# A fused attention and gated feed-forward kernel on one core: four 32-row matmuls at a time on TensorE, with a written-out order for every engine

## The chip, the cores and the metric

The chip is a Trainium2 and the kernel runs on one of its cores. The metric is the time on the device in microseconds (us), the median of several executions. "Clock" is the mean TensorE clock that the hardware granted, as a share of full speed. A run is called slow when it lies over 1.5 % above the fastest run of the same kernel.

## The reference

```python
B, N, m, C = (4, 12416, 32, 128)          # batches, tokens, inducing points, channels
d_ff = 1536                                # 12 chunks of 128

def mab(q, kv):
    s = scale * (q @ kv.transpose(0, 2, 1))
    s = s - s.max(-1, keepdims=True)
    a = np.exp(s)
    a /= a.sum(-1, keepdims=True) + 1e-09
    return a @ kv
h = mab(I, x)                              # stage 1: the 32 inducing points look at all tokens
x2 = mab(x, h)                             # stage 2: every token looks at the 32 rows of h
gate = 1.0 / (1.0 + np.exp(-(x2 @ w_gate)))
val = x2 @ w_val
out = gate * val @ w_out                   # 49664 x 128
```

Both kernels use that `x2` is a product of 128 tokens' weights over only 32 rows. They fold `h @ w_gate` and `h @ w_val` once a batch into a table of 32 rows ("fold"). The gate and value matmuls then contract over those 32 rows. The sigmoid is written with tanh: gate × value = 0.5 · (tanh(g/2) + 1) · v.

## The kernel before

It goes through each batch in blocks of 512 tokens: 24 full blocks and one of 128 tokens. A step is one tanh with the work around it: six steps make a full block, each for two of the twelve 128-wide chunks of d_ff. (With the change the short block has two steps, so there are 4 × (24 × 6 + 2) = 584 in all.) This is the core of a block, with cuts marked. The contraction is padded from 32 to 128 rows with zeros, and the output is transposed by a DMA.

```python
    pp_g = ...tile_pool(name="pp_g", bufs=2, space=PSUM)   # two double banks for gates
    pp_v = ...tile_pool(name="pp_v", bufs=3, space=PSUM)   # three banks for values and everything else
    pp_acc = ...tile_pool(name="pp_acc", bufs=1, space=PSUM)
    # ... (cut)
        for p in range(NP2):                       # six steps of two chunks
            j0, j1 = 2 * p, 2 * p + 1
            g_pair = pp_g.tile([P, 2, TOK], F32, tag="g")
            nc.tensor.matmul(
                g_pair[:, 0, 0:T], hwg[:, ts(j0, P)], a2[:, 0:T], start=True, stop=True
            )
            # ... the same for j1 (cut)
            nc.scalar.activation(
                out=tgs[:, 0:2, 0:T], in_=g_pair[:, 0:2, 0:T], func=AF.Tanh, scale=0.5
            )
            for (jj, j) in ((0, j0), (1, j1)):
                v_ps = pp_v.tile([P, TOK], F32, tag="v")
                nc.tensor.matmul(
                    v_ps[:, 0:T], hwv[:, ts(j, P)], a2[:, 0:T], start=True, stop=True
                )
                nc.vector.scalar_tensor_tensor(
                    out=u[:, 0:T], in0=tgs[:, jj, 0:T], scalar=1.0,
                    in1=v_ps[:, 0:T], op0=ALU.add, op1=ALU.mult,
                )
            for (j, u) in prev_us:
                nc.tensor.matmul(
                    acc_ps[:, 0:T], wo16[:, j, :], u[:, 0:T], start=(j == 0), stop=(j == NJ - 1),
                )
            # ... one piece of the attention work of another block goes here (cut)
        nc.scalar.copy(out=outT16[:, 0:T], in_=acc_ps[:, 0:T])
        nc.sync.dma_start(onat16[:, 0:nch, :], outT16[:, 0:T], transpose=True)
```

The softmax here doesn't subtract the row's maximum and nothing guards it: scores larger than these inputs give would overflow.

Of the kernel before, what the change touches and what calls it, by code (L numbers as in the profile page):

```python
# [14 lines left out]
P = 128  # L16
TOK = 512


def _affine_eye(nc, ap, pattern, fill=1.0):  # L20
    nc.gpsimd.memset(ap, 0.0)
    nc.gpsimd.affine_select(
        out=ap,
        in_=ap,
        compare_op=ALU.not_equal,
        fill=fill,
        base=0,
        pattern=pattern,
        channel_multiplier=1,
    )  # L30
# [3 lines left out]
def kernel(  # L34
# [11 lines left out]
    m = inducing.shape[0]  # L46
    F = moe_w_gate.shape[1]
    NJ = F // P
    SCALE = float(1.0 / (C ** 0.5))

    assert C == P and m == 32 and F % P == 0 and N % P == 0

    nfull = N // TOK
    tail = N - nfull * TOK
    blocks = [(i * TOK, TOK) for i in range(nfull)]
    if tail:
        blocks.append((nfull * TOK, tail))
    nb = len(blocks)

    const = ctx.enter_context(tc.tile_pool(name="const", bufs=1))  # L60
    xTp = ctx.enter_context(tc.tile_pool(name="xTp", bufs=2))
    pers = ctx.enter_context(tc.tile_pool(name="pers", bufs=1))
    hp = ctx.enter_context(tc.tile_pool(name="hp", bufs=2))
    xab = ctx.enter_context(tc.tile_pool(name="xab", bufs=16))
    a1p = ctx.enter_context(tc.tile_pool(name="a1p", bufs=2))
    a2rp = ctx.enter_context(tc.tile_pool(name="a2rp", bufs=3))
    moep = ctx.enter_context(tc.tile_pool(name="moep", bufs=4))
    outp = ctx.enter_context(tc.tile_pool(name="outp", bufs=4))

    pp_g = ctx.enter_context(tc.tile_pool(name="pp_g", bufs=2, space=bass.MemoryType.PSUM))  # L70
    pp_v = ctx.enter_context(tc.tile_pool(name="pp_v", bufs=3, space=bass.MemoryType.PSUM))
    pp_acc = ctx.enter_context(tc.tile_pool(name="pp_acc", bufs=1, space=bass.MemoryType.PSUM))

    ident128 = const.tile([P, P], F16, tag="ident128")
    _affine_eye(nc, ident128[:], [[-1, P]])

    ind16 = const.tile([m, C], F16, tag="ind16")
    nc.gpsimd.dma_start(ind16[:], inducing)
    indT16 = const.tile([P, m], F16, tag="indT16")
    nc.sync.dma_start(indT16[:], ind16[:], transpose=True)  # L80

    wg16 = const.tile([P, F], F16, tag="wg16")
    nc.gpsimd.dma_start(wg16[:], moe_w_gate)
    wv16 = const.tile([P, F], F16, tag="wv16")
    nc.gpsimd.dma_start(wv16[:], moe_w_val)
    wo16 = const.tile([P, NJ, C], F16, tag="wo16")
    nc.gpsimd.dma_start(wo16[:], moe_w_out.rearrange("(j p) c -> p j c", p=P))

    NPAD = 3
    a2pads = [pers.tile([P, TOK], F16, name=f"a2pad{k}", tag=f"a2pad{k}") for k in range(NPAD)]  # L90
    hwgs = [pers.tile([P, F], F16, name=f"hwg{q}", tag=f"hwg{q}") for q in range(2)]
    hwvs = [pers.tile([P, F], F16, name=f"hwv{q}", tag=f"hwv{q}") for q in range(2)]
    for t_ in (*a2pads, *hwgs, *hwvs):
        nc.vector.memset(t_[m : 2 * m, :], 0.0)
        nc.vector.memset(t_[64:P, :], 0.0)

    xTs = [xTp.tile([P, N], F16, tag="xT", name=f"xT_{b}") for b in range(B)]
    h16s = [pers.tile([m, C], F16, name=f"h16_{b}", tag=f"h16_{b}") for b in range(B)]
    hT16s = [pers.tile([P, m], F16, name=f"hT16_{b}", tag=f"hT16_{b}") for b in range(B)]
    haccs = [pers.tile([m, C + 4], F32, name=f"hacc_{b}", tag=f"hacc_{b}") for b in range(B)]  # L100
    for b in range(B):
        nc.vector.memset(haccs[b][:], 0.0)

    x16nats = {}
    a1s = {}

    def x16nat_load(b, kk):
        t0, T = blocks[kk]
        nch = T // P
        x16nat = xab.tile([P, 4, C + 4], F16, tag="x16nat")  # L110
        nc.gpsimd.dma_start(  # L111
            x16nat[:, 0:nch, 0:C],
            x[b, ds(t0, T)].rearrange("(j p) c -> p j c", p=P),
        )
        nc.vector.memset(x16nat[:, 0:nch, C : C + 1], 1.0)
        x16nats[(b, kk)] = x16nat

    def st1_a(b, kk, pe_xt):
        t0, T = blocks[kk]
        nch = T // P  # L120
        x16nat = x16nats[(b, kk)]
        xt_ps = pp_v.tile([P, TOK], F16, tag="v")
        for j in range(nch):
            nc.tensor.transpose(xt_ps[:, ts(j, P)], x16nat[:, j, 0:C], ident128[:])  # L124
        if pe_xt:
            nc.vector.tensor_copy(out=xTs[b][:, ds(t0, T)], in_=xt_ps[:, 0:T])
        else:
            nc.scalar.copy(out=xTs[b][:, ds(t0, T)], in_=xt_ps[:, 0:T])

    def st1_b(b, kk):  # L130
        t0, T = blocks[kk]
        nch = T // P
        s1_ps = pp_v.tile([P, 4, m], F32, tag="v")
        for j in range(nch):
            nc.tensor.matmul(  # L135
                s1_ps[:, j, :],
                xTs[b][:, ds(t0 + j * P, P)],
                indT16[:],
                start=True,
                stop=True,  # L140
            )
        a1 = a1p.tile([P, 4, m], F16, tag="a1")
        nc.scalar.activation(
            out=a1[:, 0:nch, :], in_=s1_ps[:, 0:nch, :], func=AF.Exp, scale=SCALE
        )
        a1s[(b, kk)] = a1

    def st1_c(b, kk):
        t0, T = blocks[kk]
        nch = T // P  # L150
        x16nat = x16nats.pop((b, kk))
        a1 = a1s.pop((b, kk))
        hpp = pp_v.tile([m, C + 1], F32, tag="v")
        for j in range(nch):
            nc.tensor.matmul(  # L155
                hpp[:],
                a1[:, j, :],
                x16nat[:, j, 0 : C + 1],
                start=(j == 0),
                stop=(j == nch - 1),  # L160
            )
        nc.vector.tensor_tensor(
            out=haccs[b][:, 0 : C + 1],
            in0=haccs[b][:, 0 : C + 1],
            in1=hpp[:],
            op=ALU.add,
        )

    def ab_end0(b):
        rec = hp.tile([m, 1], F32, tag="rec")  # L170
        nc.vector.reciprocal(out=rec[:], in_=haccs[b][:, C : C + 1])
        nc.vector.tensor_scalar_mul(
            out=h16s[b][:], in0=haccs[b][:, 0:C], scalar1=rec[:]
        )
        hT_ps = pp_v.tile([P, m], F16, tag="v")
        nc.tensor.transpose(hT_ps[:], h16s[b][:], ident128[0:m, 0:m])
        nc.vector.tensor_copy(out=hT16s[b][:], in_=hT_ps[:])

    def ab_fold(b, q):
        hwg, hwv = hwgs[b % 2], hwvs[b % 2]  # L180
        npg = F // TOK
        (dst, w, sc) = (hwg, wg16, None) if q < npg else (hwv, wv16, 0.5)
        ss = q % npg
        hw_ps = pp_v.tile([m, TOK], F32, tag="v")
        nc.tensor.matmul(
            hw_ps[:], hT16s[b][:], w[:, ts(ss, TOK)], start=True, stop=True
        )
        if sc is None:
            nc.vector.tensor_copy(out=dst[0:m, ts(ss, TOK)], in_=hw_ps[:])
        else:  # L190
            nc.vector.tensor_scalar_mul(  # L191
                out=dst[0:m, ts(ss, TOK)], in0=hw_ps[:], scalar1=sc
            )

    a2ns = {}

    def st2_a(b, i):
        t0, T = blocks[i]
        nch = T // P
        s2_ps = pp_v.tile([P, 4, m], F32, tag="v")  # L200
        for j in range(nch):
            nc.tensor.matmul(  # L202
                s2_ps[:, j, :],
                xTs[b][:, ds(t0 + j * P, P)],
                hT16s[b][:],
                start=True,
                stop=True,
            )
        a2r = a2rp.tile([P, 4, m], F16, tag="a2r")
        nc.scalar.activation(  # L210
            out=a2r[:, 0:nch, :], in_=s2_ps[:, 0:nch, :], func=AF.Exp, scale=SCALE
        )
        sums_tok = a2rp.tile([P, 4], F32, tag="sums_tok")
        nc.vector.reduce_sum(out=sums_tok[:, 0:nch], in_=a2r[:, 0:nch, :], axis=AX.X)
        rtok = a2rp.tile([P, 4], F32, tag="rtok")
        nc.vector.reciprocal(out=rtok[:, 0:nch], in_=sums_tok[:, 0:nch])  # L216
        a2n = a2rp.tile([P, 4, m], F16, tag="a2n")
        nc.gpsimd.tensor_tensor(  # L218
            out=a2n[:, 0:nch, :],
            in0=a2r[:, 0:nch, :],  # L220
            in1=rtok[:, 0:nch].unsqueeze(2).to_broadcast((P, nch, m)),
            op=ALU.mult,
        )
        a2ns[(b, i)] = a2n
# [196 lines left out]
```

## Time and profile before

| | before |
|---|---|
| median of 2 runs | 970.2 us (969.97 to 970.43) |
| span of the profiled run, clock | 967.2 us, 0.986 |
| busy: PE / DVE / ACT / POOL | 96 % / 88 % / 73 % / 20 % |
| chain that ended last | PE 92 % |

The engines are PE (TensorE's matmuls), PEld (its weight loads), DVE (VectorE), ACT (ScalarE), POOL (GpSimd) and SP (which issues DMAs). These are lines of the page of the kernel before: the busy line, the clock in 40 slices of the span (tenths of full speed), the chain that ended last by engine, and the largest groups. In a group, the first figures after the bar are the busy us and the mean ns of one instruction. Then come the idle us before them and what ended most of that idleness.

```profile
span 967.2 us, 16308 instructions
...
PE 932.7 (96%) x5568; PEld 423.7 (44%) x5568; DVE 855.0 (88%) x1779; ACT 701.6 (73%) x976; POOL 195.4 (20%) x310
...
PEclk9899999999999999999999999999999999999998
...
PE 92%; DVE 4%; DMA 1%; ACT 1%; issue 1%; POOL 1%; POOLq 0%; ACTq 0%; DVEq 0%
...
L264 DVE SCALAR_TENSOR_TENSOR u<-tgs,v_ps 128x512 f16<-128x512 f16 (+1 forms) x1200 | 746.5, 666 | 76.9 <-PE v_ps L260 37.6
L254 ACT ACTIVATE tgs<-g_pair 128x1024 f16<-128x1024 f32 x600 | 592.4, 1004 | 184.9 <-PE g_pair L250 126.5
L274 PE MATMUL acc_ps<-u,wo_104 128*128 128x512 f16 (+1 forms) x1000 | 357.4, 374 | 0.0
```

PE is busy throughout at nearly full clock, and the chain that ended last runs through it. The 374 ns of the output matmul are not its cost, since matmuls overlap in the pipeline. The cost is the distance between the starts. This is the timeline of PE (start, duration, engine, line, operation, out<-in):

```profile
501.44 0.38 PE L247 MATMUL g_pair<-a2pad_108,hwg_110 128*128 128x512 f16 x1
501.66 0.38 PE L260 MATMUL v_ps<-a2pad_108,hwv_112 128*128 128x512 f16 x1
```

The starts of such neighbours are 0.215 to 0.216 us apart in the whole trace. A block has 36 such matmuls, so 7.8 us of its some 9.4 us are these alone, although three quarters of the rows of the gate and value matmuls are zeros.

### The profile page before, as it was taken

How to read it: one execution, taken by the hardware profiler on the slowest of the kernel's cores; microseconds unless marked ns; L12 is line 12 of the kernel's file. 1: busy time of each engine (PE TensorE's matmuls, PEld its weight loads, DVE VectorE, ACT ScalarE, POOL GpSimd, SP SyncE). 2: the span in 40 equal slices, each digit the busy share in tenths (PEclk: the TensorE clock that was granted, in tenths of full speed). 3: DMA queues.
4: the chain of work that ended last, by engine and by line, in shares of the span. 5: the costliest groups of instructions: out<-in, count | busy, mean ns of one | idle time of the engine just before them, and what ended most of it. 6: DMA issues, size and time to landing. Idle time of an engine off the chain costs nothing.

```text
span 967.2 us, 16308 instructions
## 1 busy us (share of the span) xinstructions
PE 932.7 (96%) x5568; PEld 423.7 (44%) x5568; DVE 855.0 (88%) x1779; ACT 701.6 (73%) x976; POOL 195.4 (20%) x310
## 2 busy tenths in 40 slices
PE   4799999999989999999998999999998999999996
PEld 3444444444444444444444444444443544444443
DVE  6799889898889889898898988898888899999996
ACT  1277787777857787777866787777775787888884
POOL 8511221212211221212221121211110111111111
PEclk9899999999999999999999999999999999999998
DMA  9924434445533434444451435423232233233333
GB/s 152 118 36 53 61 50 57 58 52 66 64 40 45 61 50 56 61 52 63 61 66 27 55 51 59 56 39 45 39 45 34 37 50 49 39 50 49 47 48 54
DMA packets 157428, 53.12 MB, mean 55 GB/s; under 512 B 107424, under 2 KB 157088, under 8 KB 157344
## 3 DMA queue, kind: packets, MB, share of 16 engines
q0 software_dynamic: 104416, 39.34, 34.8%
q1 hardware_dynamic: 52928, 12.74, 7.3%
q8 instruction: 43, 0.70, 0.3%
q14 instruction: 41, 0.34, 0.1%
HBM read 27.80 MB, written 25.43 MB: 55 GB/s over the span
## 4 chain that ended last, share of the span: by engine, by line
PE 92%; DVE 4%; DMA 1%; ACT 1%; issue 1%; POOL 1%; POOLq 0%; ACTq 0%; DVEq 0%
PE v_ps L260 27%; PE acc_ps L274 21%; PE g_pair L247 15%; PE g_pair L250 13%; PE acc_ps L285 4%; PE a2nT_ps L233 3%; PE hpp L155 3%; PE xt_ps L124 2%; DVE u L264 2%; PE s_ps L135 2%; DMA x16nat<-in_x_dram 1%; PE s_ps L202 1%; ACT tgs L254 1%; DVE hwv_111 L191 0%; DVE hwv_112 L191 0%
## 5 line engine op out<-in xcount | busy, mean ns | idle before, releaser
L264 DVE SCALAR_TENSOR_TENSOR u<-tgs,v_ps 128x512 f16<-128x512 f16 (+1 forms) x1200 | 746.5, 666 | 76.9 <-PE v_ps L260 37.6
L254 ACT ACTIVATE tgs<-g_pair 128x1024 f16<-128x1024 f32 x600 | 592.4, 1004 | 184.9 <-PE g_pair L250 126.5
L274 PE MATMUL acc_ps<-u,wo_104 128*128 128x512 f16 (+1 forms) x1000 | 357.4, 374 | 0.0
L218 POOL TENSOR_TENSOR a2n<-a2r,rtok 128x128 f16<-128x128 f16 (+1 forms) x100 | 38.7, 387 | 531.9 <-DVE rtok L216 527.3
L274 PEld LDWEIGHTS <-wo_104 128*128 128x128 f16 x1000 | 97.6, 98 | 106.5 <-issue 11.4
L111 POOL DMA_DIRECT2D x16nat<-in_x_dram x100 | 73.7, 747 | 56.0 <-PE hpp L155 29.6
L260 PEld LDWEIGHTS <-hwv_112 128*128 128x128 f16 x600 | 56.7, 97 | 63.5 <-issue 6.1
L260 PEld LDWEIGHTS <-hwv_111 128*128 128x128 f16 x600 | 55.6, 98 | 56.0 <-issue 5.4
L285 PE MATMUL acc_ps<-u,wo_104 128*128 128x512 f16 (+1 forms) x200 | 74.5, 373 | 1.9 <-DVE u L264 1.9
L260 PE MATMUL v_ps<-a2pad_106,hwv_111 128*128 128x512 f16 (+1 forms) x216 | 75.7, 369 | 0.0
L260 PE MATMUL v_ps<-a2pad_106,hwv_112 128*128 128x512 f16 (+1 forms) x216 | 74.9, 363 | 0.3 <-DVE u L264 0.2
L260 PE MATMUL v_ps<-a2pad_108,hwv_111 128*128 128x512 f16 x192 | 70.0, 379 | 1.0 <-DVE hwv_112 L191 0.4
L260 PE MATMUL v_ps<-a2pad_108,hwv_112 128*128 128x512 f16 x192 | 69.6, 379 | 0.6 <-DVE u L264 0.4
L260 PE MATMUL v_ps<-a2pad_107,hwv_112 128*128 128x512 f16 x192 | 69.7, 379 | 0.0
L260 PE MATMUL v_ps<-a2pad_107,hwv_111 128*128 128x512 f16 x192 | 69.6, 379 | 0.0
L124 PE MATMUL xt_ps<-ident_91,x16nat 128*128 128x128 f16 x388 | 39.3, 224 | 13.6 <-DMA x16nat<-in_x_dram 11.8
L210 ACT ACTIVATE a2r<-s_ps 128x128 f16<-128x128 f32 (+1 forms) x100 | 28.9, 289 | 28.3 <-PE s_ps L202 27.9
L124 PEld LDWEIGHTS <-x16nat 128*128 128x128 f16 x388 | 29.9, 100 | 33.6 <-DMA x16nat<-in_x_dram 12.4
L250 PEld LDWEIGHTS <-hwg_109 128*128 128x128 f16 x300 | 29.4, 98 | 33.9 <-issue 11.2
L233 PE MATMUL a2nT_ps<-ident_91,a2n 128*32 128x128 f16 x388 | 39.9, 223 | 3.8 <-POOL a2n L218 1.9
L250 PEld LDWEIGHTS <-hwg_110 128*128 128x128 f16 x300 | 29.2, 97 | 32.1 <-issue 7.0
L247 PE MATMUL g_pair<-a2pad_106,hwg_109 128*128 128x512 f16 (+1 forms) x108 | 40.6, 376 | 1.6 <-DVE a2pad_106 L234 1.3
(610 smaller groups left out, 1051.3 us busy)
## 6 DMA issues: line engine op xcount, KB each, us to landing
x16nat<-in_x_dram POOLq DMA_DIRECT2D x96, 128.0 KB, 3.3
wg_100<-in_moe_w_gate_dram POOLq DMA_DIRECT2D x1, 384.0 KB, 4.7
wv_102<-in_moe_w_val_dram POOLq DMA_DIRECT2D x1, 384.0 KB, 6.0
wo_104<-in_moe_w_out_dram POOLq DMA_DIRECT2D x1, 384.0 KB, 7.7
out_dram<-onat_856 POOLq DMA_DIRECT2D x1, 256.0 KB, 2.6
out_dram<-onat_971 POOLq DMA_DIRECT2D x1, 256.0 KB, 2.7
out_dram<-onat_1108 POOLq DMA_DIRECT2D x1, 256.0 KB, 2.6
out_dram<-onat_1245 POOLq DMA_DIRECT2D x1, 256.0 KB, 2.6
```

What stands on the lines that cost most here:

```text
L111: nc.gpsimd.dma_start(x16nat[:, 0:nch, 0:C], x[b, ds(t0, T)].rearrange("(j p) c -> p j c", p=P),)
L124: nc.tensor.transpose(xt_ps[:, ts(j, P)], x16nat[:, j, 0:C], ident128[:])
L155: nc.tensor.matmul(hpp[:], a1[:, j, :], x16nat[:, j, 0 : C + 1], start=(j == 0), stop=(j == nch - 1),)
L218: nc.gpsimd.tensor_tensor(out=a2n[:, 0:nch, :], in0=a2r[:, 0:nch, :], in1=rtok[:, 0:nch].unsqueeze(2).to_broadcast((P, nch, m)), op=ALU.mult,)
L233: nc.tensor.transpose(a2nT_ps[:, ts(j, P)], a2n[:, j, :], ident128[:])
L247: nc.tensor.matmul(g_pair[:, 0, 0:T], hwg[:, ts(j0, P)], a2[:, 0:T], start=True, stop=True)
L250: nc.tensor.matmul(g_pair[:, 1, 0:T], hwg[:, ts(j1, P)], a2[:, 0:T], start=True, stop=True)
L254: nc.scalar.activation(out=tgs[:, 0:2, 0:T], in_=g_pair[:, 0:2, 0:T], func=AF.Tanh, scale=0.5)
L260: nc.tensor.matmul(v_ps[:, 0:T], hwv[:, ts(j, P)], a2[:, 0:T], start=True, stop=True)
L264: nc.vector.scalar_tensor_tensor(out=u[:, 0:T], in0=tgs[:, jj, 0:T], scalar=1.0, in1=v_ps[:, 0:T], op0=ALU.add, op1=ALU.mult,)
L274: nc.tensor.matmul(acc_ps[:, 0:T], wo16[:, j, :], u[:, 0:T], start=(j == 0), stop=(j == NJ - 1),)
L285: nc.tensor.matmul(acc_ps[:, 0:T], wo16[:, j, :], u[:, 0:T], start=(j == 0), stop=(j == NJ - 1))
```

## The change

The intent is to take the load off TensorE. Four tables of 32 rows lie one under the other, and four matmuls (two gate chunks and two value chunks of different steps) run at once in the four row groups of the array: a "session". The output matmuls are turned round, so that `u` is stationary and the outputs come with tokens on partitions. This drops the output's transpose. One of twelve gated products goes to POOL, after ACT has copied its values out of PSUM. From the second batch on, the transposes of x go from PE to DMA. A planner in the program, run when it is built, models each engine and each PSUM bank and fixes every engine's order in advance. (PSUM is the memory that the matmuls of both kernels write into. A value bank holds 512 columns, a gate bank is a double one.) The file is written anew, so this shows only the core of the difference, with cuts marked:

```diff
-            nc.tensor.matmul(
-                g_pair[:, 0, 0:T], hwg[:, ts(j0, P)], a2[:, 0:T], start=True, stop=True
-            )
+                        PE.matmul(t[:, (c - lo) * P * nt : (c - lo + 1) * P * nt], lhsT=h[32 * k : 32 * k + 32, c * P : (c + 1) * P],
+                                  rhs=rows(k), start=c == lo + k * per, stop=c == lo + (k + 1) * per - 1,
+                                  tile_position=(32 * k, 0), skip_group_check=True)
 ... (k = 0, 1: the gates' row groups; the values, in groups 2 and 3:)
+            rg = 2 + m % 2
+            key = 1000 + LEAD + m // 2 + (0.05 if m % 2 == 0 else 0.3)
+                    PE.matmul(psl("V", o)[:, i * P * nt : (i + 1) * P * nt], lhsT=h[32 * rg : 32 * rg + 32, F + c * P : F + (c + 1) * P],
+                              rhs=rows(rg), start=i == 0, stop=i == len(cs) - 1, tile_position=(32 * rg, 0), skip_group_check=True)
 ...
-                nc.tensor.matmul(
-                    acc_ps[:, 0:T], wo16[:, j, :], u[:, 0:T], start=(j == 0), stop=(j == NJ - 1),
-                )
+                for j in range(nt):
+                    PE.matmul(PSA[0][:, j * P : (j + 1) * P], lhsT=ub.t[:, o0 + j * P : o0 + (j + 1) * P], rhs=wo[:, c, :],
+                              start=n == 0 and j == 0, stop=n == len(order) - 1, skip_group_check=True)
 ...
+    COPIES = ((1,),)             # chunk 1 of each full block: copied by ACT, multiplied by POOL
+                    POOL.tensor_tensor(out=pt.t[:], in0=tg.t[:, t0 : t0 + TOK], in1=vs.t[:], op=ALU.mult)
+                    POOL.tensor_tensor(out=ub.t[:], in0=pt.t[:], in1=vs.t[:], op=ALU.add)
 ... (the planner's banks, and a score's claim on one of them:)
+    POOLS = {"G": 2, "V": 3, "A": 1}
+        s = op("PE", 0.3 if big else 0.23, key, deps, mode="C", need=["G"], emit=em, name=nm)
+        e = act(w + extra, key - 1.5, [s] + dst.old, give=[(s, "G")], emit=ex, name="X" + nm)
 ... (when the planner thinks that the first loads have landed; the jobs' places:)
+        lm = landed(ld, max(0.1, arrive[0] - 0.6 * i))
+        at[tuple(j)] = 1000 + st + 0.6
+    order = schedule(ops, POOLS)
```

The attention work of the next blocks and batches is cut into "jobs", at most one to a block. `s1` are the scores of stage 1 and `s2` those of stage 2 for four blocks. Each takes a gate bank for 512 or 640 columns, and an exp on ACT then reads the bank. `hp` is the weighted sum of stage 1: it takes a value bank, and DVE adds it up. `fold` makes the table. A job is placed at the one step between the output matmuls of two blocks.

## The prediction

> **What bounds the kernel now.** TensorE. The page's busy line gives PE 96%, DVE 88%, ACT 73%, POOL 20%; the chain that ended last is 92% PE; in the windows at 160–260 and 300–400 us PE is busy throughout. In the list of groups a 512-column matmul shows 379 ns, but neighbours start 216 ns apart in the timeline, so the 36 matmuls of a 512-token block cost 7.8 of about 9.4 us. The rest is transposes (56 ns apart), scores, the second attention stage, waits, and changes of array shape (309 ns instead of 216 before a 32-column transpose: +93 ns). The first gate matmul starts at 44 us.
>
> **What the change does.**
> 1. Gate and value matmuls contract over 32 rows only, so it runs two gate and two value chunks at once in four row groups. The Trainium skill (TensorE: Matmul & The Clock Gate, Part 3) states 3.07x for four such tiles: an estimate of 0.28 us in place of 4 x 0.216. No run here shows it yet. Six sessions a block, each with two shape changes: 6 x 0.47 = 2.8 us. (TensorEngine Tiling, Key Properties, says that a mode change drains the array; the +93 ns agrees.)
> 2. Output matmuls turn round: u is stationary, 48 matmuls of 128 columns at 56 ns (the pitch of the transposes, whose weight load is the same) = 2.7 us. The output's DMA transpose goes.
> 3. The next batch's x transposes go from PE and ACT to DMA; softmax sums and scaling to POOL; scores come four tiles at once. PE falls to about 5.7 us a block.
> 4. DVE: 11 of 12 gated products (604 ns apart back to back) = 6.64 us, plus 0.1 us of small work. In exchange ACT copies one value chunk (0.47 us) and POOL does that product (2.6 us, estimated from 394 ns per 128 columns).
> 5. ACT: six tanh (903–920 ns apart) 5.5 us, two 512-column copies 0.93, exps 0.25: 6.7 us.
> 6. Each engine's order is fixed in the program.
>
> **Critical path.** The bound moves from PE (9.4 us a block) to DVE and ACT, nearly equal at 6.7. With 584 steps the floor is 1.12 us a step = 654 us. Two equally loaded engines fed through two gate buffers and three value banks in a fixed order will not both stay full; the copy step loads ACT with 1.4–1.8 us and DVE with 0.6. I put 3–7% on it: 1.15–1.20 us a step, 672–700 us. The prologue loads batch 0 in 32-bit form and casts on chip: first gate at about 36 us; draining and last store 10, launch 3.
>
> **Predicted: 722 us, 692 to 755 in 8 of 10.** Faster by over 2%: 0.97; within 2%: 0.02; slower: 0.01.
>
> **What would show the steps.** Busy line: DVE 93–96%, ACT (its records overlap) over 95%, POOL 50–55%. The chain by engine is no longer 90% PE but a mix of DVE, ACT and PE. Output matmuls start 56 ns apart, a session's four within 0.1 us, with 0.1 us lost at each shape change. DVE's products stay near 604 ns apart. DVE's idle time is mostly ended by value matmuls and tanh, a few hundred ns a block.
>
> **What would make it wrong.** Row groups not overlapping (a session of 0.5 us or more makes PE the bound again: 760 us or more); POOL's product or the long row chain (DMA transposes, a trip through DRAM) arriving late and stalling the fixed order; DVE slowed while POOL works; POOL at double my estimate; a lower granted clock with PE less busy; a prologue bound by the loads (over 45 us).

## The result and the profile after

| | before | after |
|---|---|---|
| median of 2 runs | 970.2 us (969.97 to 970.43) | 779.6 us (779.23 to 779.94) |
| ratio of the fast runs | | 0.8038 (95 %: 0.8014 to 0.8061) |
| span of the profiled run, clock | 967.2 us, 0.986 | 778.2 us, 0.967 |
| busy: PE / DVE / ACT / POOL | 96 / 88 / 73 / 20 % | 88 / 89 / 90 / 44 % |
| chain that ended last | PE 92 % | PE 50 %, issue 16 %, POOL 12 %, ACT 10 %, DVE 9 % |
| first gate matmul starts | 44 us | 53.5 us |

A ratio here is the mean time of one kernel's fast runs over that of the other's fast runs in the same rounds, so it is not quite the ratio of the medians. The kernel's result is correct against the reference. The time fell by 20 %, but it lies above the range of 692 to 755 us that was predicted. These are the lines of the page after that answer to those above:

```profile
span 778.2 us, 20470 instructions
...
PE 684.4 (88%) x7851; PEld 369.7 (48%) x7851; DVE 692.4 (89%) x1157; ACT 698.7 (90%) x883; POOL 339.2 (44%) x448
...
PEclk9758999999999999999999999999999999999999
...
PE 50%; issue 16%; POOL 12%; ACT 10%; DVE 9%; DMA 2%; ACTq 0%; POOLq 0%; DVEq 0%
...
L234 DVE SCALAR_TENSOR_TENSOR u<-tga,v 128x512 f16<-128x512 f16 x1068 | 663.4, 682 | 44.7 <-PE v L234 32.0
L234 ACT ACTIVATE tga<-g 128x1024 f16<-128x1024 f32 x584 | 579.8, 1039 | 31.9 <-PE v L234 8.1
...
L234 PE MATMUL acc<-wo,u 128*128 128x128 f16 x4656 | 349.9, 222 | 0.7 <-ACT os L234 0.7
L234 POOL TENSOR_TENSOR pt<-tga,vs 128x512 f32<-128x512 f16 x96 | 111.8, 1164 | 354.3 <-ACT vs L234 346.9
...
L234 POOL TENSOR_TENSOR u<-pt,vs 128x512 f16<-128x512 f32 x96 | 121.7, 1267 | 7.6
```

PE needs 684 us instead of 933, so TensorE is no longer the one bound. ACT, DVE and PE now share the span nearly equally, and none is full. DVE idled little before its products, and value matmuls ended most of that idleness.

This is the timeline of PE in a step of an undisturbed stretch. The groups "v", "g x2", "v" are one session, and "acc" are the output matmuls:

```profile
402.70 0.39 PE L234 MATMUL v<-a2r,hw 32*128 32x512 f16 x1
402.73 0.39 PE L234 MATMUL g<-a2r,hw 32*128 32x512 f16 x2
402.74 0.38 PE L234 MATMUL v<-a2r,hw 32*128 32x512 f16 x1
403.06 0.84 PE L234 MATMUL acc<-wo,u 128*128 128x128 f16 x12
```

The four matmuls here start within 0.04 us of each other, and where nothing is waited for each comes 3 to 4 ns after the one before it. In such sessions the output matmuls begin 0.33 us after the session's start. Inside an acc group the starts are 56 ns apart. Into a session the distance is 152 ns instead of 56, so one change of the array's shape costs some 96 ns. If the 0.33 us hold one such change on the way out, the four matmuls themselves take about 0.23 us (an estimate), hardly longer than the 0.216 us that one of them took before. Most sessions are not like these, though: of the 510 in which four such matmuls stand alone, 166 start within 0.1 us, and half of them need more than 0.16 us, because a bank is waited for in between.

The four terms of the prediction's sum, against the trace of after (the end of the last tanh is at 771.3 us):

| term | predicted | measured | difference to the middle |
|---|---|---|---|
| until the first gate matmul | 36 | 53.5 | +17.5 |
| the 584 steps, to the end of the last tanh | 672–700 | 717.8 (1.229 us a step) | +31.8 |
| draining, last store | 10 | 6.9 | −3.1 |
| launch (time less span of this run, 779.94 us) | 3 | 1.7 | −1.3 |
| sum | 721–749 (middle 735) | 779.9 | +44.9 |

So two terms are to be explained: 17 us before the first gate and 32 us in the steps. The centre, 722, was moreover 13 us below the middle of its own sum.

To look into the steps, I took the time of each block from the trace, as the distance from one ACT copy of the output to the next. I sorted the blocks by the job that falls into them. A block counts as "at full clock" when at most 5 % of its neighbouring output matmuls start more than 85 ns apart, because at half clock they stand further apart (106 to 107 ns instead of 56 in this trace). The short blocks and the first of each batch are left out.

| block of after | blocks (at full clock) | median us of those at full clock |
|---|---|---|
| with s1 / s2 scores | 18 (18) / 22 (22) | 7.38 / 7.38 |
| with hp | 18 (17) | 7.33 |
| with a fold | 9 (9) | 7.40 |
| with hT (the end of stage 1) | 3 (1) | 7.83; the two slowed ones 8.9 and 9.1 |
| with no job | 22 (21) | 6.86 |

A block without a job takes 6.86 us, that is 1.14 us a step and nearly the 6.7 us that the prediction gave as the floor. A block with a job takes about 0.5 us more, and most blocks of the first three batches have one. (One block in each of the first three batches has no job and still takes 8.1 to 8.5 us. In it a small DVE reciprocal of the stage-2 chain stands in DVE's order until POOL's sums arrive, 3.1 us in all. In the run below without POOL's product the same blocks take 7.2 to 7.3 us. So the late row chain that the prediction named as a risk is real, and costs about 4 us.) In a block without a job DVE, ACT and PE are busy for 6.74, 6.59 and 6.42 us (medians). In an hp block ACT is busy 6.81 and DVE 7.07 us, in an s2 block ACT 7.26 us of 7.38. Those sums alone look as if the engine with the job's work were full.

The timeline of a block with an s2 job shows something else. The end of a line, in brackets, gives the idle time before it and what released it:

```profile
407.82 0.40 PE L234 MATMUL g<-xT,hT 128*32 128x512 f16 x4
408.04 1.13 ACT L234 ACTIVATE tga<-g 128x1024 f16<-128x1024 f32 x1
...
408.15 0.38 PE L234 MATMUL v<-a2r,hw 32*128 32x512 f16 x1
...
409.23 0.39 PE L234 MATMUL g<-a2r,hw 32*128 32x512 f16 x2 [0.69 <-ACT tga L234]
...
409.23 0.38 PE L234 MATMUL v<-a2r,hw 32*128 32x512 f16 x1
```

The score matmuls (407.82) take one of the two gate banks. The next gate matmuls need the other bank, which the tanh from 408.04 is still reading. TensorE keeps its order and waits 0.69 us for that tanh, and the second value matmul of the step, which needs nothing of this, stands behind the gates until 409.23. Added up over a block with scores, PE waits some 0.73 us for a tanh, and DVE waits 0.46 to 0.49 us, mostly for value matmuls, where it waits 0.10 in a block without a job. An hp block differs: there PE waits 0.53 us for a DVE product that frees a value bank. These waits are what the following experiments are about.

### The profile page after: what moved, and what is told of

Its sections match the earlier page's. It is cut to its first block, busy times and chain, and to the rows that moved or that the text cites. A ratio compares the mean times of both kernels' runs of the same rounds, so it can differ in the third digit from the quotient of the medians.

```text
span 778.2 us, 20470 instructions
## 1 busy us (share of the span) xinstructions
PE 684.4 (88%) x7851; PEld 369.7 (48%) x7851; DVE 692.4 (89%) x1157; ACT 698.7 (90%) x883; POOL 339.2 (44%) x448
## 4 chain that ended last, share of the span: by engine, by line
PE 50%; issue 16%; POOL 12%; ACT 10%; DVE 9%; DMA 2%; ACTq 0%; POOLq 0%; DVEq 0%
PE acc L234 26%; PE v L234 20%; DVE u L234 7%; ACT tga L234 6%; POOL u L234 4%; POOL pt L234 4%; PE g L234 4%; ACT os L234 2%; POOL tree L234 2%; POOL a2n L234 2%; DMA a<-eT 2%; DVE x L234 1%; DMA ind<-in_inducing_dram 1%; ACT xT L234 1%; ACT eT L234 0%
## 5 line engine op out<-in xcount | busy, mean ns | idle before, releaser
L234 DVE SCALAR_TENSOR_TENSOR u<-tga,v 128x512 f16<-128x512 f16 x1068 | 663.4, 682 | 44.7 <-PE v L234 32.0
L234 ACT ACTIVATE tga<-g 128x1024 f16<-128x1024 f32 x584 | 579.8, 1039 | 31.9 <-PE v L234 8.1
L234 PE MATMUL v<-a2r,hw 32*128 32x512 f16 (+1 forms) x1200 | 338.9, 379 | 21.0 <-DVE u L234 20.6
L234 PEld LDWEIGHTS <-u 128*128 128x128 f16 x4656 | 266.4, 99 | 183.0 <-issue 181.7
L234 PE MATMUL acc<-wo,u 128*128 128x128 f16 x4656 | 349.9, 222 | 0.7 <-ACT os L234 0.7
L234 POOL TENSOR_TENSOR pt<-tga,vs 128x512 f32<-128x512 f16 x96 | 111.8, 1164 | 354.3 <-ACT vs L234 346.9
L234 PE MATMUL g<-a2r,hw 32*128 32x512 f16 (+1 forms) x1200 | 230.2, 383 | 32.7 <-ACT tga L234 32.0
L234 PEld LDWEIGHTS <-hw 32*128 32x128 f16 x2400 | 70.4, 91 | 139.6 <-issue 87.0
L234 POOL TENSOR_TENSOR u<-pt,vs 128x512 f16<-128x512 f32 x96 | 121.7, 1267 | 7.6
L234 ACT COPY os<-acc 128x512 f32<-128x512 f32 (+1 forms) x100 | 58.2, 582 | 3.3 <-PE acc L234 3.3
```

Source lines behind the costliest of these rows:

```text
L234: return chain(fn(*a, **k), self.name)
```

## The experiments

The runs were made on one chip each, with the kernel before beside them (medians 969.5 to 970.3 us). First the theories, with the letters that the expectations use. A: the extra half us of a job block is a wait that TensorE's fixed order makes, by the job's instructions in that order or by the PSUM bank that a job takes. Its rival, B: it is the job's work on ACT and DVE, which the prediction averaged in as 0.25 us a block. For the prologue: the loads, a slow DVE cast beside POOL, or the planned order itself.

### The new kernel again, as a control

> The changed kernel itself, unchanged, on the chip of the next three, as their reference: 778 to 781 us, first gate matmul at 53 to 54 us, blocks with a score or second stage 7.3 to 7.4 us, without 6.86.

Measured: 777.54 us (774.92 to 781.08), ratio 0.8015 (0.7984 to 0.8045), first gate at 53.0 us. Blocks with s1 or s2 take 7.38, with hp 7.33, with a fold 7.39, with none 6.85 us. This and the first measurement of the same kernel agree to 0.3 %, and the runs scatter by 0.8 %. Differences of a few us have to be read from the blocks and not from the totals.

### One scaling in the prologue moved from POOL to ACT

These are the lines of the prologue of after that the theory came from. A cast of 1024 columns on DVE takes 6.36 us while POOL casts (from 24.04) and scales (from 26.04), against 0.68 us for the same cast alone:

```profile
24.36 6.36 DVE L234 CAST x<-xT 128x1024 f16<-128x1024 f32 x1
...
26.04 4.12 POOL L234 TENSOR_SCALAR wo<-tga 128x1536 f16<-128x1536 f32 x1
...
36.43 0.68 DVE L234 CAST x<-xT 128x1024 f16<-128x1024 f32 x1
...
53.50 1.03 PE L234 MATMUL g<-a2r,hw 32*128 32x512 f16 x4 [0.52 <-DVE a2r L234]
```

```diff
-    wl["wo"] = op("POOL", 3.0, 40, ..., emit=lambda o: POOL.tensor_scalar(out=wo..., in0=WS[2], scalar1=0.5, ...))
+    wl["wo"] = act(F, 40, ..., emit=lambda o: ACT.mul(out=wo..., in_=WS[2], mul=0.5))
```

> One op of the prologue moves: the scaling of the output weights goes from POOL to ACT. In the changed kernel's timeline a DVE cast of batch 0 took 6.36 us instead of 0.68, from 24.36 us on, exactly while POOL cast and scaled. Theory: [...] this stall is on the prologue's critical path: that cast falls to 0.7 us, the first gate matmul comes at about 48 us instead of 53.5, time about 774 us. Rival: the prologue is bound by the loads or by the planned order of the later casts: first gate within 2 us of before, 778 to 780 us.

Measured: 774.94 us (774.15 to 777.96), ratio 0.7998, first gate at 52.6 us. The cast at 24.2 us now took 2.25 us, so its length did come from POOL's work beside it. (The Trainium skill, GPSIMD Engine Reference, section 1 "Specifications", says that POOL's SBUF interfaces are shared with VectorE, which agrees.) But the first gate came only 0.9 us earlier. The last cast on DVE still waited behind a copy of the scores of an earlier quarter of x, which was at 35.23 us. The theory fell: the long cast is real and off the deciding path. That the total met the expected 774 us is no support: the control's own runs reach down to 774.9.

### The planned order of the prologue, with landing times from the trace

In the trace of after, the loads run mostly at 400 to 440 GB/s and have landed at about 24 us, with the last cast at 36 us. The planner's model lets the later quarters of x land much later after their issue than they did, and it fixed the order of DVE, ACT and PE by that. This run gives the planner the landing times that the trace shows (and keeps the scaling on ACT):

```diff
-        lm = landed(ld, max(0.1, arrive[0] - 0.6 * i))
+        lm = landed(ld, max(0.1, arrive[0] - 0.6 * i) if i < 3 else 9.0)
 # likewise: the last rows of x 9.1, the gate and value weights 10.3, the output weights 13.7, inducing points 6.0
```

> Moving the weight scaling off POOL alone brought the first gate forward by only 0.9 us (52.6): my stall theory fell, because DVE's last cast still stood in its fixed order behind work of the quarter before it, though the loads had been done at about 24 us. This run gives the planner the landing times that the trace shows (9.0 us after issue for the later loads of x, 10.3 and 13.7 for weights, 6 for the inducing points), and leaves the scaling on ACT. Theory (the planned order of the prologue is the cause): first gate at 42 to 46 us, time 767 to 772 us against a control of 779. Rival (chain of dependences and cold TensorE clock, whatever the order): first gate at 50 us or later, 776 or more.

Measured: 767.59 us (766.23 to 768.88), ratio 0.7913, ten us below the control beside it. The blocks are unchanged (7.38 and 6.85 us). The first gate matmuls in this run:

```profile
42.58 0.60 PE L234 MATMUL g<-a2r,hw 32*128 32x512 f16 x4 [0.53 <-DVE a2r L234]
```

42.6 us instead of 53.0 in the control: the theory held. About 10 of the 17.5 us are a planned order that rested on wrong landing times. The remaining 6.6 us, against the 36 of the prediction, stay in one piece.

### All four matmuls of a session in one row group

```diff
-   lhsT=h[32 * k : 32 * k + 32, ...], rhs=rows(k), tile_position=(32 * k, 0)      # gates; values likewise
+   lhsT=h[0:32, ...], rhs=rows(0), tile_position=(0, 0)
```

> All four matmuls of a session go to row group 0 (the operands are there four times over, so the result stays right). Nothing else changes. Theory: running four row groups at once is what took TensorE off the bound: a session goes from about 0.32 us to 4 x 0.216 = 0.86, TensorE's least work per block from 5.6 to 8.8 us, a block to 8.9 to 9.6 us, time 910 to 980 us, most of the gain gone. Rival: the gain came from the work taken off TensorE (transposes by DMA, turned output matmuls) and the concurrency is mostly hidden: under 850 us.

Measured: 1709.2 us (1708.91 to 1709.24), ratio 1.7627, result correct. That is outside both expectations, and the reason is in the windows. The columns are the window, then for each engine the busy us (and its instructions), the clock, the share of DMA and GB/s:

```profile
core 0: us, PE busy (x) PEld busy (x) DVE busy (x) ACT busy (x) POOL busy (x), PEclk, DMA share, GB/s
400.00:500.00 100.00, 100.00 (x451) 44.50 (x450) 44.67 (x66) 46.81 (x54) 17.91 (x21) 0.50 0.11 33
```

PE is busy by its records for all of these 100 us, and the granted clock is 0.50. Blocks took 16.5 to 17.5 us. The run therefore mixes two causes. As an estimate, half of that, 8.2 to 8.8 us, would be a block at full clock, near the expected 8.8. It supports that the row groups are what makes a session short, but it is no clean measurement of that. What it shows cleanly is the clock: TensorE shows no idle time and ran at half clock. (The ends of matmuls are modelled in the profile, so short idleness could be hidden.)

### Both value matmuls in one row group, the gates as they were

This was the milder form of the same question.

```diff
-   lhsT=h[32 * rg : 32 * rg + 32, F + ...], rhs=rows(rg), tile_position=(32 * rg, 0)
+   lhsT=h[64:96, F + ...], rhs=rows(2), tile_position=(64, 0)
```

> Both value matmuls of a session in row group 2, so the second can only start 0.216 us after the first; result right, DVE and ACT unchanged. Theory A (TensorE's in-order chain sets the block): sessions grow from 0.32 to about 0.53 us, a block by 0.5 to 1.2 us, time 830 to 890 us, the granted clock as before. Theory B (DVE and ACT set it): within 8 us of 778. A falling clock, as in the run with one row group (0.51), would make it longer still and would mix two causes.

Measured: 811.21 us (801.07 to 813.83, the highest a slow run), ratio 0.8315. Blocks take 7.66 with s1, 7.53 with hp, 7.66 with s2 and 7.03 with none, so 0.2 to 0.3 us more each. Three blocks take about 12 us where the clock dips (mean clock 0.951). The direction is that of theory A, but the time lies outside both expectations: six more times 0.216 us on TensorE are mostly hidden, which fits a TensorE that is no longer the bound.

### Five of twelve output chunks not computed (wrong)

```diff
             def em(o, n=n, c=c, ub=ub, o0=o0):
+                if n % 2 == 1 and n != len(order) - 1:
+                    return
                 for j in range(nt):
```

> Wrong result on purpose: 5 of the 12 output chunks of a block are not multiplied, 20 matmuls of 56 ns = 1.1 us less TensorE work per block, no change for DVE and ACT. Theory A (TensorE's fixed order with three value banks couples the engines; TensorE is late by its own work plus waits): blocks with a job (scores, second stage, fold) fall from 7.36 to about 6.9 us, those without from 6.86 to about 6.7, time about 745 us. Theory B (DVE's and ACT's own load sets the 7.36): time within 8 us of 779.

Measured: 779.93 us (776.27 to 790.23; the fast runs 776.3 to 781.4), ratio 0.8031. Nothing was won in total. By the total alone that would be theory B. But the fast runs had a clock of 0.846 to 0.865, against 0.967 in after: TensorE had less to do and was granted less. The profile fell into the one slow run (788.5 us, clock 0.816). There, the blocks at full clock take 7.09 to 7.10 with scores, 6.69 with hp and 6.69 with none, and the slowed ones 7.6 to 8.6. So at full clock TensorE's output matmuls seem to cost the job blocks 0.3 to 0.6 us; that comes from a slow run and is only a support. The total stayed where it was, at the lower clock.

### No value copy, all twelve products on DVE

```diff
-    COPIES = ((1,),)
+    COPIES = ((),)
```

> All 12 gated products of a block on DVE, no value chunk copied by ACT, no product on POOL. By my prediction (DVE sets the pace) a block costs 12 x 0.604 + 0.1 = 7.35 us against 6.75: about 50 us longer. Theory A (job blocks are held at 7.36 by TensorE's order anyway): only the blocks without a job lengthen, by 0.4 to 0.5 us, time 785 to 795 us.

Measured: 783.71 us (781.96 to 784.98), ratio 0.8076, against 779.6 in the first measurement of the kernel after and 777.5 in the control. Blocks with s1 take 7.38, with hp 7.47, with a fold 7.38, with none 7.17 us. In the blocks without a job the exchange is worth 0.32 us, in those with hp 0.14, in those with scores nothing. In all it is worth some 4 to 6 us, where the prediction's arithmetic (0.6 us of DVE a block, 96 blocks) would make it some 50. So in the blocks with scores or a fold the load of DVE is not what sets the time. Where there is no job it is: with all twelve products DVE is busy for 7.17 of 7.17 us, twelve times the 598 ns between two products. In an hp block it is busy for 7.46 of 7.47.

### The job's exp cut to 32 of its 512 columns (wrong)

```diff
         def ex(o):
             t = psl("G", s)
+            if key >= 1000:
+                ACT.activation(out=dst.t[:, 0:32], in_=t[:, 0:32], func=AF.Exp, scale=SCALE)
+                return
```

> Wrong result on purpose: in the main loop each score's exp on ACT covers 32 of 512 columns, 0.2 us instead of 0.5 to 0.7; TensorE and DVE are as before. Theory B (ACT's load sets the blocks with a score): these fall from 7.38 to 6.9 us, 17 to 20 us less in all. Theory A (TensorE's order): they stay at 7.25 to 7.35, like the second-stage blocks that have no ACT work, 2 to 6 us less.

Measured: 778.40 us (775.67 to 778.51), ratio 0.8018. ACT's records in an s2 block fell from 7.26 to 6.85 us, and the blocks still take 7.38. Theory B, that ACT's work sets these blocks, fell.

### No job work at all, its place in the plan kept (wrong)

The matmuls of the scores and of hp, the exps and the additions are not issued. The planner still plans all of them. The folds stay.

```diff
+            if key >= 1000:
+                return                        # in the scores' matmuls and in the exps
-               emit=lambda o: hpp_mm(o, psl("V", o), b, i, a_b, buf, True, True))
+               emit=lambda o: None)          # hp; likewise its addition on DVE
```

> Wrong result on purpose: in the main loop the score matmuls, their exp, the second-stage matmuls and their DVE addition are not issued (folds and the transposes by DMA stay). Theory A: the blocks that had such a job fall from 7.3 to 7.4 us to 6.85, the figure of the blocks that never had one, 26 to 30 us less: 748 to 753 us, unless the granted clock falls with less TensorE work as it did when output matmuls were left out (0.82 to 0.87). Rival (the 7.38 us come from transfers or POOL work of that time): within 10 us of 778.

Measured: 796.09 us (790.48 to 796.39), ratio 0.8195: slower than with the work. Blocks at full clock take 7.22 to 7.41 us by job and batch, the same as with it (the median difference, block by block, is 0.00 us). 22 blocks are slowed, most to 8.4 to 8.8 us, with a mean clock of 0.933. My expectation of 6.85 us failed, and with it theory A in its first form, that the job's instructions in TensorE's order cost the time. The place of an s1 job at 262.5 us, in a trace in which no score is issued:

```profile
262.57 1.04 ACT L234 ACTIVATE tga<-g 128x1024 f16<-128x1024 f32 x1
...
263.67 0.39 PE L234 MATMUL g<-a2r,hw 32*128 32x512 f16 x2 [0.86 <-ACT tga L234]
```

The gate matmuls wait 0.86 us for the tanh of 262.57, as in the kernel after, though nothing has been written into any bank in between. The plan had given the next gate bank to the score that isn't there, so the gates of two following steps got the same bank.

### Neither the work nor the bank (wrong)

The same, and the planner gives the jobs no bank:

```diff
-        s = op("PE", ..., mode="C", need=["G"], emit=em, name=nm)
+        s = op("PE", ..., mode="C", need=["G"] if key < 1000 else [], emit=em, name=nm)
 # likewise need=[] and give=[] of hp and its addition, give=[] of the exps
```

> Wrong result on purpose: as the run without jobs, but the jobs reserve no bank in the plan either. Bank theory: at full clock the blocks that stayed at 7.3 to 7.4 us without any job work fall to 6.85 to 7.1 us. Otherwise (transfers, POOL work or the next batch's stage slow these batches): they stay at 7.3 or more. The granted clock may dip as before, so blocks at full clock are compared, not the total.

Measured: 760.14 us (757.66 to 762.81), ratio 0.7828. The blocks that had scores or hp take 7.10 us in batch 0 and 7.03 us in batches 1 and 2, at full clock, where the run before had 7.39, 7.31 and 7.38. The four s2 blocks of the last batch fell from 7.28 to 6.85. The blocks of the last batch without a job stay at 6.85. From the first output copy to the last of the full blocks it took 687.7 us, against 706.1 in after. So removing the bank took 0.28 to 0.35 us off the blocks of the first three batches and 0.43 off those four, where removing the work had taken nothing. Some 0.2 us over 6.85 are left in the first three batches. This is the place of the same s1 job as above, now without a wait for a tanh:

```profile
253.37 0.37 PE L234 MATMUL v<-a2r,hw 32*128 32x512 f16 x1 [0.23 <-DVE u L234]
253.38 0.39 PE L234 MATMUL g<-a2r,hw 32*128 32x512 f16 x2
```

### The bank alone, without any work, where there was no job

The reverse: in the last batch's blocks without a job, the planner gives a gate bank to a matmul and an exp that are never issued. The result is correct.

```diff
+    for st in free:
+        if st > gfirst[B - 1, 0]:
+            key = 1000 + st + 0.6
+            p = op("PE", 0.23, key, [], mode="C", need=["G"], emit=lambda o: None, name="phantom")
+            p.strict = True
+            act(512, key - 1.5, [p], give=[(p, "G")], emit=lambda o: None, name="Xphantom")
```

> In the last batch each free step without a job gets a phantom: it reserves a gate bank in the plan for as long as a job would, and issues no instruction at all. Result right. Bank theory: these blocks go from 6.85 to 7.2 or 7.3 us, about 17 of them, 6 to 8 us more than the control of 777.5. Otherwise: 6.85 as before, total unchanged.

Measured: 794.64 us (792.18 to 796.79), ratio 0.8189. No instruction was added, and those blocks went from 6.85 to 7.24–7.28 us at full clock. Six of the nineteen were slowed to 8.45 us or more, with the mean clock at 0.948 and, in the last batch, 0.93 instead of 0.98. The stretch from the first output copy to the last of the full blocks is 722.3 us, 16 more than in after. As an estimate, nineteen times 0.43 us, some 8 of them, are the bank, and the rest came with the clock. A phantom also books the time of a job in the plan. But the four s2 blocks of this batch in the run before had that booking and no bank, and took 6.85 us: it is the bank. First a step of after at the place where the phantom will be, then the same place in this run:

```profile
651.19 0.37 PE L234 MATMUL v<-a2r,hw 32*128 32x512 f16 x1 [0.23 <-DVE u L234]
651.20 0.39 PE L234 MATMUL g<-a2r,hw 32*128 32x512 f16 x2
```

```profile
655.25 0.37 PE L234 MATMUL v<-a2r,hw 32*128 32x512 f16 x1 [0.23 <-DVE u L234]
656.57 0.39 PE L234 MATMUL g<-a2r,hw 32*128 32x512 f16 x2 [0.95 <-ACT tga L234]
656.58 0.39 PE L234 MATMUL v<-a2r,hw 32*128 32x512 f16 x1
```

In after, gates and value go on together at 651.19. With the bank reserved, a value matmul goes at 655.25, the gates wait 0.95 us for a tanh and the next value waits behind them.

### Jobs placed before the session of their step

If the bank's wait is the cause, a place where its tanh ends sooner should help. The score moves from after the session of the free step to before it:

```diff
-        at[tuple(j)] = 1000 + st + 0.6
+        at[tuple(j)] = 1000 + st + 0.02
```

> Jobs (scores, second stage, fold) go in front of the session of the free step instead of behind it; the same work on every engine. Theory A (TensorE's order and the banks that a job takes cost the time): blocks with a score fall from 7.38 to 7.1 or 7.25 us, with a second stage from 7.33 to about 7.25, time 769 to 774 us. Theory B (load of ACT and DVE in such a block): no change, within 3 us of the control.

Measured: 768.96 us (766.17 to 777.11), ratio 0.7941, against 777.5 for the control beside it. Blocks with scores take 7.22 and 7.23, with hp 7.13, with a fold 7.37, with none 6.89 us. The stretch of blocks takes 692.0 us instead of 705.1. With the same work, some 0.2 us a job (13.1 us over 67 jobs) are won by the place alone. The totals scatter by 11 us here, so the blocks are the evidence. The jobs' matmuls now come just before the output copy that divides the blocks, so part of a job's cost can fall into the block after it. In the trace, gates behind a score now wait 0.53 us for the score's exp, where they had waited 0.69 us for a tanh.

### Two value banks instead of three

```diff
-    POOLS = {"G": 2, "V": 3, "A": 1}
+    POOLS = {"G": 2, "V": 2, "A": 1}
```

> Two value banks instead of three, nothing else. Theory A (the second value matmul of a session waits for its bank and holds TensorE with it): blocks 8.2 to 8.9 us, time 860 to 890 us. Rival (the banks are not what couples the engines): within 15 us of 778.

Measured: 920.28 us (912.91 to 923.49), ratio 0.9479. At full clock the blocks take 7.92 with none, 8.28 with s2, 8.49 with s1 and 8.89 with hp, with a mean clock of 0.921. It is slower than expected, and of the gain of 20 % only 5 % are left with one bank less; part of that came with the lower clock. (The Trainium skill, TensorEngine Tiling (Array Packing), "Gotcha 1: PSUM Pressure", says that row tiling raises the pressure on PSUM, since different row tiles write different banks. No run here shows what row tiling adds to it; what one bank less costs this kernel is 7.92 against 6.86 us a block without a job.)

### Prologue order and early jobs together

> The two working edits together: the prologue's landing times in the planner with the scaling on ACT, and jobs ahead of the session of the free step. If the two gains are independent (10 us and 13 us less span in the profiles of the single runs): first gate near 43 us, 753 to 760 us. If jobs placed early only shift waits elsewhere: 763 or more.

The edits are those of the prologue and of the early jobs. Measured: 753.25 us (752.15 to 755.39), ratio 0.7770 (0.7755 to 0.7785), correct, clock 0.979. The first gate comes at 42.5 us, the stretch of blocks takes 690.2 us, and blocks with scores take 7.22, with hp 7.13, with none 6.90. Against the kernel after it is 0.777 / 0.8038 = 0.967, so 3.3 % faster. The two gains add up, and it is the best version.

## Why the prediction was right or wrong

**Right: the bound leaves TensorE.** Four matmuls in four row groups start within 0.01 us where nothing is waited for, output matmuls stand 56 ns apart, and a shape change costs 96 ns, where 93 was read from the trace of before. (The Trainium skill, TensorEngine Tiling, "Key Properties", says that a change of the mode drains the array, and the trace agrees.) PE's busy time fell from 933 to 684 us. In the blocks without a job PE's records fill 6.42 of 6.86 us, more than the 5.7 predicted. But a record is longer than what its matmul costs: 379 ns, where neighbours started 216 ns apart. The session was even cheaper than the estimate, 0.23 us instead of 0.28. What did not come is "a session's four within 0.1 us" as the rule: only 166 of 510 did.

**Right: the products.** DVE's products back to back start 598 ns apart (604 predicted), with POOL at work beside them or not: they last 680 to 681 ns either way. POOL's product took 1.164 + 1.267 = 2.43 us (2.6 predicted). The busy shares of the page came out lower than predicted (DVE 89 %, ACT 90 %, POOL 44 %), because the span is longer; DVE's 692 us would be 96 % of 722.

**Wrong, the step "first gate at about 36 us": it was 53.5.** I had not looked at how the planner models the loads. It lets the later quarters of x land long after they did, and the fixed order of the engines follows that. With landing times from the trace the first gate came at 42.6 us and the total fell by 10 us: shown by that run. The loads themselves were not the bound, though 53.5 us is past the "over 45" that the prediction named for that case: they had landed at about 24 us. The other 6.6 us lie somewhere on the way from the last casts over the scores, the sums, the table, the first stage-2 scores, their scaling and their transposes. That was not split further. In that stretch the clock is low (the second to fourth of the 40 slices of after show 7, 5 and 8 tenths), and the first four gate matmuls last 1.03 us in after and 0.60 in the run with the other order. What the low clock costs there was not separated.

**Wrong, the step "I put 3–7% on it: 1.15–1.20 us a step": it was 1.229.** The mechanism as such, two equally loaded engines fed through few banks in a fixed order, was named, and without a job it cost only 2 % (6.86 against 6.7). What I mis-sized is the job. I had counted jobs as work, with exps of 0.25 us averaged over the blocks. The runs show that their work hardly matters and their bank does. An exp cut to 32 of 512 columns changed nothing, and no work at all changed nothing. Giving the bank back took 0.28 to 0.43 us off a block, and reserving a gate bank without any work added 0.39 to 0.43. A job takes one of two gate banks (or of three value banks) in a fixed order. After scores the following gates then need the bank whose tanh is running, TensorE waits 0.7 to 0.95 us for it in order, and a value matmul that DVE needs stands behind. As an estimate, the 67 blocks with scores, hp or a fold lie 34 us above 6.86 us each. The steps took 64 us more than the floor of 654, where the middle of the forecast allowed 32: 34 by the jobs and 13 by the 2 % of every block. The other 16 or so are in the blocks with hT, those at half clock and the three that wait for POOL's sums, and were not tested.

**Wrong, the arithmetic: 722 stood for a sum of 735.** Its own terms give 721 to 749. I had put the centre at the lower end of what I had added up.

**"A lower granted clock with PE less busy" was named as a risk, and it is real.** It cost after little (0.967 against 0.986). But with fewer output matmuls the fast runs had 0.846 to 0.865 and nothing was won, and 22 blocks without job work and six with a phantom lost about 1 us or more each to it. That less work on PE is its cause is not shown. The run without work and bank issues the same instructions as the one without work, and was granted 0.962 to 0.975 where that one had 0.931 to 0.939. The phantom run issues all the work, and had 0.948 to 0.959.

**Left open.** Blocks with neither work nor bank still took 7.03 to 7.10 us and not 6.85 in the first three batches. The planner still books the time of those jobs, but the four s2 blocks of the last batch, booked too, took 6.85. So the rest may lie in what only the first three batches have (loads, transposes by DMA, more work on POOL); that is argued, not shown. The phantom tested a gate bank. A value bank for hp was not tested alone, and the folds, which were issued in every run, were not tested at all. What sets the granted clock is open too.

## What to carry to other kernels

When a change frees an engine and fixes every engine's order, count the PSUM banks a side job occupies and for how long, not just its work: a bank taken at the wrong step made the following matmuls wait for the reader of the other bank, and everything behind them in order waited too. Where a program plans with modelled times, put the landing times of a trace into the model before anything else; here that was 10 us for a handful of numbers. Read experiments that change TensorE's work or its waits together with the granted clock, because it changed with them here (0.51 to 0.98).

## What the Trainium skill lacked or had wrong

- TensorE: Matmul & The Clock Gate, Part 1 ("What's actually happening") and "Why this matters for your kernels": half clock is put down to idleness, and keeping TensorE busy for 4 us or more is said to bring the full clock. Here PE's records fill 100 of 100 us and the granted clock is 0.50 when all gate and value matmuls sit in one row group. The page has no such case. (The ends of these records are modelled, so they do not exclude short idleness.)
- TensorE: Matmul & The Clock Gate, Part 3 ("Measured speedup vs the span model"): the 3.07x for four tiles of 32 rows fits neither way of counting here. By estimate, four matmuls took about 0.23 us against 4 x 0.216, near 3.8x, and about 0.42 us, near 2x, with the shape change of some 96 ns on each side, for which no page gives a figure. Its starts of about 4 ns apart agree with the 3 to 4 ns here.
- No page that I read has a figure for a PSUM bank reserved in a fixed order without any work: 0.39 to 0.43 us a block here.
